# q and k of two token chunks by seven block products instead of eight, and the gate's logits out of v's products, on one core

## Chip, core and metric

The kernel runs on one core of a Trainium2 chip. The core has five engines with an instruction queue each: TensorE (PE in the profile; its weight loads are PEld), VectorE (DVE), ScalarE (ACT), GpSimd (POOL), and SyncE (SP), which here only issues DMAs. Each queue runs strictly in order, and semaphores tie the queues to each other. The metric is the device time of one execution in microseconds, median over several runs.

## What is computed

Input x has 2048 tokens of D = 448 features. Two branches are mixed token by token by a gate:

```python
g = sigmoid((x * gate_w).sum(-1, keepdims=True))
# branch A: attention over 8 keys, offsets 0, 2, .. 14 back; 16 heads of 28
q, k, v = split(x @ wqkv)                      # 448 x 1344
idx  = pos[:, None] - arange(8) * 2            # masked where < 0
o    = softmax(q . k[idx] * 28**-0.5) . v[idx]
a    = o @ wo
# branch B
b = relu(x @ w1 + b1)**2 @ w2 + b2             # 448 -> 1792 -> 448
return g * a + (1 - g) * b
```

All is fp32.

## The kernel before

Every fp32 product is made of three products in TensorE's faster 32-bit format: each operand is split into a high part (a rounded copy, on ScalarE) and a low part (raw minus high, on VectorE; `split_full`, L115 and L116), and hi x hi, hi x lo, lo x hi are summed in PSUM. The contraction over 448 features is three full blocks of 128 rows and an end of 64 rows (tiles `x7`, `x8`, weights `w7h`, `w7l`).

The matmuls run as pairs of 64-row halves of the array, side by side (`side_by_side`, L186): the two halves work on different accumulators at the same time. A block of 128 rows so takes one half product on the lower rows and one on the upper rows. An accumulator that has gathered the rows of one half must be handed to the other half; between the two a "turn" stands (`turn`), an operation on one element of the PSUM bank (memset on VectorE, L196, or a copy on ScalarE, L194) which waits for the first half's matmuls and for which the other half's matmuls wait.

Tokens come in four chunks of 512 (four tiles of 128). For each chunk TensorE makes q, k and v. Chunk 0 (`qkv_first`): 36 matmuls over full rows for q (L255), 48 pairs for the rest of q and for k, 42 pairs for v; v's turns stand after 24 pairs (v0, v1) and after 33 (v2, v3), counted as they are needed. Chunks 1 to 3: `qkv_two` twice, for two token tiles each, 63 pairs. Results go from PSUM into stage tiles on ScalarE (`qkv_evacuate`, L205, two token tiles to a stage tile, three stage tiles in all) and from there by DMA (L211) to q_d, k_d and v_d in DRAM. From there GpSimd's attention loads them (from 70.9 us on, products L335 and L342 on GpSimd, sums L336 and L350 on VectorE), while TensorE goes on with branch B ("h" and "b" matmuls) and at the end with the output product ("a").

The gate's logits are made on VectorE: for each chunk four multiplications of x's raw blocks by the gate's weights (L682, L680), a transposition (L686) and a sum (L687); they go through a small DRAM tile once.

The order of all instructions is fixed in the code: `when(t, ...)` puts a step in at an estimated time t (ns, of a clock that `advance` moves on with each group of matmuls), and steps that are due are written into the engines' queues between the matmuls. So what stands before what on an engine follows from these numbers. SP issues all DMAs in one queue; each issue also waits for the landing of the one eight places before it.

Of the kernel before, what the change touches and what calls it, by code (L numbers as in the profile page):

```python
# [14 lines left out]
P = 128  # L15
NS = 8
# [7 lines left out]
NQ = D + 2  # L24
NZ = 64
NP = 512
# [31 lines left out]
def gated_mix_kernel(ctx: ExitStack, tc: tile.TileContext, xT, wqkv, w1, w2, wo, b1, b2, out):  # L58
# [11 lines left out]
    z_d = tc.dram_tile([P, NZ], F32, name="z_d")  # L70
# [10 lines left out]
    w1h = const.tile([P, 3, F], F32R, name="w1h")  # L81
    w1l = const.tile([P, 3, F], F32R, name="w1l")
# [8 lines left out]

    xpool = ctx.enter_context(tc.tile_pool(name="xpool", bufs=1))
# [5 lines left out]
    zg = smallp.tile([P, 6, NS], F32, name="zg")  # L98
    zt, gt, g1t = zg[:, 0:2], zg[:, 2:4], zg[:, 4:6]
# [54 lines left out]
    wqh = ap.tile([P, 3, NP + 2 * D], F32R, name="wqh")  # L154
    wql = ap.tile([P, 3, NP + 2 * D], F32R, name="wql")

    w7h = ap.tile([P, NP + D], F32R, name="w7h")
    w7l = ap.tile([P, NP + D], F32R, name="w7l")
# [3 lines left out]
    nc.gpsimd.memset(halo0, 0.0)  # L162

    stage = {}

    def block(b):

        o = (0, NP, NP + D)[b]
        return slice(o, o + D)
# [29 lines left out]
    def qkv_evacuate(pt, c, tl, b):  # L199
        par, t = c // 2, (c % 2) * 4 + tl  # L200
        first = (b, t // 2) not in stage
        if first:
            stage[b, t // 2] = xap.tile([P, G, 2, C], F32, tag="stage", name=f"st{c}_{tl}_{b}", bufs=ST_BUFS)
        st = stage[b, t // 2]
        nc.scalar.activation(st[:, :, t % 2], pt[:, :D].rearrange("p (g c) -> p g c", g=G), AF.Copy)  # L205
        if not first:
            stage.pop((b, t // 2))
            t0 = t - t % 2
            dst, off = ((q_d, 0), (k_d, HALO), (v_d, HALO))[b]
            dd = dst[par, :, off:off + SP].rearrange("g (p s) c -> p g s c", s=NS)[:, :, t0:t0 + 2]  # L210
            nc.sync.dma_start(dd.rearrange("p g s c -> p g (s c)"), st.rearrange("p g s c -> p g (s c)"))  # L211
# [9 lines left out]
    def last(x, acc, tl, b):  # L221

        sl = slice(tl * P, tl * P + P)
        n = block(1) if b == 2 else slice(0, D)
        h, l = w7h[:, n], w7l[:, n]
        return [(acc, x.x7[:, sl], h), (acc, x.x7[:, sl], l), (acc, x.x8[:, sl], h)]

    def accs(c, b, tls, tags):
        return [Acc(t, f"qkv{c}_{tl}_{b}", D) for t, tl in zip(tags, tls)]
# [60 lines left out]


# [101 lines left out]
    def gates(par):  # L393

        e = smp.tile([P, 32], F32, tag="e", name=f"e{par}")[:, :NS]
        nc.scalar.activation(e, zt[:, par], AF.Exp, scale=-1.0)
# [127 lines left out]
    def w1_piece(i, dt, gap):  # L524
# [74 lines left out]
    def h_turn(accs, f):  # L599
        touch(w1h[:, 2].rearrange("p (f n) -> p f n", n=P)[:, f:f + 2, 0:1])  # L600
# [35 lines left out]

    raws = [raw_tile("wqraw0")]
    rx = raw_tile("xraw0")
    for k in range(4):
        if k < 3:  # L640
            nc.sync.dma_start(raws[0][:, k, :NQ], wqkv[0, :, k])
        else:
            for b, rows in ((0, slice(0, 64)), (1, slice(64, P))):
                nc.sync.dma_start(raws[0][rows, k, :NQ], wqkv[b, rows, k])
# [3 lines left out]
    for b, tag in ((1, "k"), (2, "v")):  # L648
        raw = attp.tile([P, 3, D], F32, tag=tag, name=f"wqraw{b}")
        for k in range(3):  # L650
            nc.sync.dma_start(raw[:, k], wqkv[b, :, k, :D])
        raws.append(raw)
    raw7 = attp.tile([P, D], F32, tag="q", name="wqraw7")
    nc.sync.dma_start(raw7, wqkv[2, :, 3, :D])
# [16 lines left out]
    zs = smp.tile([P, 3, NZ], F32, tag="lg", name="zs")  # L671
    zu = xcp.tile([P, CH], F32, tag="zu", name="zu")
    zpart, zall, gw = zs[:, 0], zs[:, 1], zs[:, 2, 0:4]
    nc.vector.tensor_copy(gw, raws[0][:, :, D])

    def z_product(raw, k):

        r = slice(0, P if k < 3 else 64)
        if k:
            nc.vector.scalar_tensor_tensor(zu[r], raw[r, k], gw[r, k:k + 1], zu[r], op0=ALU.mult, op1=ALU.add)  # L680
        else:
            nc.vector.tensor_scalar_mul(zu, raw[:, 0], gw[:, 0:1])  # L682

    def z_sums(c):

        nc.vector.transpose(zu, zu)  # L686
        nc.vector.tensor_reduce(  # L687
            zpart.rearrange("p (b c t) -> p c t b", b=4, c=4)[:, c],
            zu.rearrange("p (t b r) -> p t b r", t=4, b=4), axis=AX.X, op=ALU.add)

    def z_store():

        nc.sync.dma_start(z_d, zpart)

    def z_load():

        for b in range(4):
            nc.sync.dma_start(
                zall[b * 32:b * 32 + 32].rearrange("p (a n) -> p a n", a=4),
                z_d[:, b * 16:b * 16 + 16].rearrange("(a c) n -> c a n", a=4))  # L700

    def z_last():

        nc.vector.tensor_reduce(
# [516 lines left out]
```

## Time and profile before

| what | value |
|---|---|
| median of 3 runs | 413.39 us (413.04 to 413.75) |
| span of the profiled execution | 412.0 us; the page gives no other time of it, its runs' median is 1.4 us above |
| PE busy | 407.8 us, 99%, clock granted in full throughout |
| DVE, ACT, POOL busy | 270.6 (66%), 210.4 (51%), 268.4 (65%) us |
| DMA | 73.83 MB, mean 179 GB/s over the span |
| q, k, v of chunk 0 on PE | 4.34 to 31.28 us |
| all of q, k, v on PE | until 104.76 us, the last chunk mixed with other work from then on |

A row of the timeline reads: start, duration (of several instructions from the first's start to the last's end), engine, line, operation, output tile <- input tiles, shapes, count, and in brackets the idle time of the engine before it and what ended that. A row of the windows reads: stretch, its length, busy time and count of each engine, TensorE's clock, the DMA engines' busy share, GB/s.

### The profile page before, as it was taken

The numbers are of one execution on the slowest core, as the hardware profiler recorded it, in microseconds if no ns is written. First come the engines' busy times: TensorE is split into PE (matmuls) and PEld (weight loads), VectorE is DVE, ScalarE is ACT, GpSimd is POOL, SyncE is SP. The second block draws the span as 40 slices with busy tenths as digits, with TensorE's granted clock in tenths as the row PEclk, the third lists the DMA queues.
The fourth block names the chain that finished last, engine by engine and source line by source line (L and its number), as shares of the span: only waits on it lengthen the run. The fifth ranks groups of instructions, "written<-read, shape, count | busy, mean of one in ns | idle before, by whom it ended". The sixth has DMA issues, their size and how long they took to land.

```text
span 412.0 us, 9331 instructions
## 1 busy us (share of the span) xinstructions
PE 407.8 (99%) x3835; PEld 366.0 (89%) x3835; DVE 270.6 (66%) x430; ACT 210.4 (51%) x461; POOL 268.4 (65%) x167
## 2 busy tenths in 40 slices
PE   8999999999999999999999999999999999999997
PEld 7999999999888888888888888989898888888996
DVE  4590745276767766787656798879576677892354
ACT  4641646387775555444565535444653254346540
POOL 0000001955999999989989899999899977940000
PEclk9999999999999999999999999999999999999999
DMA  7999999979262315654112649765146530168304
GB/s 213 368 351 309 286 390 288 355 223 315 91 241 99 128 51 209 208 186 152 41 47 105 222 158 270 196 146 154 28 157 200 217 130 2 45 179 132 95 0 181
DMA packets 66763, 73.83 MB, mean 179 GB/s; under 512 B 33120, under 2 KB 59296, under 8 KB 66464
## 3 DMA queue, kind: packets, MB, share of 16 engines
q1 hardware_dynamic: 66720, 73.23, 55.4%
q8 instruction: 30, 0.49, 0.5%
q14 instruction: 13, 0.11, 0.1%
HBM read 45.74 MB, written 28.28 MB: 180 GB/s over the span
## 4 chain that ended last, share of the span: by engine, by line
PE 99%; DVE 0%; issue 0%
PE b L186 33%; PE h L186 32%; PE qkv L186 23%; PE a L186 7%; PE qkv L255 2%; PE warm L634 1%; PE a L993 1%; PE last L993 0%; DVE bt L872 0%; PE last L985 0%; PE a L985 0%; DVE zero L631 0%; DVE b1z L632 0%
## 5 line engine op out<-in xcount | busy, mean ns | idle before, releaser
L335 POOL TENSOR_TENSOR qk<-q,k 128x896 f32<-128x896 f32 x64 | 135.2, 2144 | 84.2 <-DMA k<-k_d 76.0
L342 POOL TENSOR_TENSOR av<-lg,v 128x896 f32<-128x896 f32 x64 | 119.2, 1957 | 6.2 <-DVE lg L336 5.6
L621 DVE TENSOR_TENSOR h<-h,h 128x512 fp32r<-128x512 f32 x56 | 38.4, 688 | 66.8 <-ACT h L624 66.5
L186 PE MATMUL qkv<-wqh,x 64*128 64x448 f32 x528 | 78.2, 359 | 0.0
L336 DVE TENSOR_REDUCE lg<-qk 128x32 f32<-128x896 f32 x64 | 67.0, 1074 | 0.0
L350 DVE TENSOR_REDUCE o<-av 128x112 f32<-128x896 f32 x64 | 66.4, 1070 | 0.1
L186 PE MATMUL b<-w2ah,h 64*128 64x448 f32 x448 | 66.3, 359 | 0.0
L186 PE MATMUL b<-w2bh,h 64*128 64x448 f32 x448 | 66.1, 359 | 0.0
L622 ACT ACTIVATE h<-h,b1z 128x512 f32<-128x512 f32 x56 | 36.7, 655 | 43.6 <-PE h L186 43.6
L186 PEld LDWEIGHTS qkv<-wqh,x 64*128 64x128 f32 x528 | 49.4, 184 | 3.6
L186 PE MATMUL qkv<-wql,x 64*128 64x448 f32 x264 | 47.7, 358 | 0.0
L186 PEld LDWEIGHTS b<-w2bh,h 64*128 64x128 f32 x448 | 42.1, 184 | 3.5
L186 PEld LDWEIGHTS b<-w2ah,h 64*128 64x128 f32 x448 | 42.0, 184 | 3.7
L205 ACT ACTIVATE st<-qkv 128x448 f32<-128x448 f32 x48 | 23.5, 542 | 34.3 <-PE qkv L186 31.7
L186 PE MATMUL b<-w2bl,h 64*128 64x448 f32 x224 | 40.7, 358 | 0.0
L186 PE MATMUL b<-w2al,h 64*128 64x448 f32 x224 | 40.5, 358 | 0.0
L623 ACT ACTIVATE h<-h 128x512 fp32r<-128x512 f32 x56 | 33.5, 598 | 1.7
L624 ACT ACTIVATE h<-h 128x512 f32<-128x512 f32 x56 | 33.3, 594 | 0.0
L573 ACT ACTIVATE h<-h 128x4 fp32r<-128x4 f32 (+1 forms) x35 | 7.2, 207 | 44.4 <-PE b L186 44.2
L186 PE MATMUL h<-x2b,w1h 64*128 64x512 f32 x168 | 28.1, 386 | 0.0
L186 PE MATMUL h<-x,w1h 64*128 64x512 f32 x168 | 28.1, 386 | 0.0
L186 PE MATMUL h<-x1b,w1h 64*128 64x512 f32 x168 | 28.1, 386 | 0.0
(150 smaller groups left out, 688.6 us busy)
## 6 DMA issues: line engine op xcount, KB each, us to landing
k<-k_d SPq DMA_DIRECT2D x8, 840.0 KB, 5.6
v<-v_d SPq DMA_DIRECT2D x8, 840.0 KB, 5.0
x_d<-x SPq DMA_DIRECT2D x11, 512.0 KB, 6.8
q_d<-st SPq DMA_DIRECT2D x8, 448.0 KB, 5.5
k_d<-st SPq DMA_DIRECT2D x8, 448.0 KB, 5.2
v_d<-st SPq DMA_DIRECT2D x8, 448.0 KB, 5.8
w1raw<-w SPq DMA_DIRECT2D x4, 896.0 KB, 9.2
q<-q_d SPq DMA_DIRECT2D x8, 448.0 KB, 3.6
```

The source lines that it names most:

```text
L186: nc.tensor.matmul(acc.pt[:, :acc.n], a[rows], w[rows], start=acc.todo == acc.all, stop=acc.todo == 1)
L205: nc.scalar.activation(st[:, :, t % 2], pt[:, :D].rearrange("p (g c) -> p g c", g=G), AF.Copy)
L255: nc.tensor.matmul(acc.pt[:, :D], a, w, start=k == j == 0, stop=False)
L335: nc.gpsimd.tensor_mul(pr, q[:, s:s + 1].to_broadcast([P, W, C]), k[:, s:s + W])
L336: pending.append(lambda: nc.vector.tensor_reduce(lg[:, s], pr.rearrange("p w (h d) -> p w h d", h=HG), axis=AX.X, op=ALU.add))
L342: nc.gpsimd.tensor_mul(pr.rearrange("p (h d) w -> p w h d", h=HG), lg[:, s][:, :, :, None].to_broadcast([P, W, HG, DH]), v[:, s:s + W].rea ...
L350: nc.vector.tensor_reduce(o[:, g * C:(g + 1) * C], pr, axis=AX.X, op=ALU.add)
L573: nc.scalar.activation(ap, f32(ap), AF.Copy)
L621: nc.vector.tensor_sub(hl, pt, f32(hh))
L622: ops += [lambda pt=pt, r=r: nc.scalar.activation(pt, pt, AF.Relu, bias=b1t[:, f + r:f + r + 1]), lambda pt=pt, hh=hh: nc.scalar.activatio ...
L623: lambda pt=pt, hh=hh: nc.scalar.activation(hh, pt, AF.Square),
L624: lambda pt=pt, r=r, low=low: (nc.scalar.activation(pt, pt, AF.Square), at(delays[r], low))]
```

## The change

For chunks 1 and 2, q and k of two token tiles are made together by Strassen's scheme. Take two token tiles (rows) and two weight blocks q and k (columns), and as the halves of the contraction the lower and the upper 64 rows of each 128-row block: a product of 2x2 blocks that takes eight block products, and by the scheme seven, of sums and differences of blocks. The sums of x's blocks (S: tiles `s`, from raw x and a second copy `xs` with its 64-row halves exchanged) and of the weights' blocks (T: from raw weights and an exchanged copy `tw`; and `t_ends` for the 64-row end) are made on chip and then split into high and low parts. T's parts lie in the tiles of w2's first part, which are free until later; S's in new half-width tiles that the second half of w1 takes later. The seven products and v's are run by `flow`, which goes through both chunks in one list with orders written by hand: each step has a half product on the lower and one on the upper rows, as the list and the accumulators' state allow. A unit of two tiles has 75 half products of q and k instead of 84; the PE queue has 468 half products in 237 steps for both chunks, six steps with one half empty (before: 504 in 252). Some results are added from PSUM to a stage tile on VectorE.

v's weights get two more columns with the gate's weights, so v's products are 450 wide in all chunks; ScalarE copies the logits' column out of PSUM, and the zu work and the way through DRAM go. Chunk 1's splits, the spills of x (x_d), w1's and w2's pieces get other times; the raw slot of x is taken ahead of that of q's weights.

The core of the diff:

```diff
-NQ = D + 2
...
+NV = D + 2
...
+    def qk_seven(c, u, x, inner):   # one unit: token tiles t[0], t[1] of chunk c; three banks X_, Y, Z
...
+        # bank, half of the rows, half products, which, waits for, gives, delay, what follows
+            one(X_, 0, 9, lambda: half_rows(0, *xt(0), *w_(0)), [], "s1", READ, lambda: copied(X_, "q", 0)),
+            one(Y, 1, 9, lambda: half_rows(1, *xt(0), *w_(0)), [], "y", TURN, lambda: turned(Y)),
+            one(Z, 0, 9, lambda: half_rows(0, *s_(1), *t_(0)), ["S"], "p5", READ, lambda: copied(Z, "k", 1)),
+            one(X_, 1, 9, lambda: half_rows(1, *s_(1), *t_(1)), ["s1", "p5"], "u2", READ, lambda: copied(X_, "k", 0)),
+            one(Y, 0, 3, lambda: ends(0, x, t[0], w7), ["y", "s1"], "c11", READ, lambda: added(Y, "q", 0), ...),
+            one(Z, 0, 3, lambda: ends(0, x, t[0], d7), ["p5"], "z", TURN, lambda: turned(Z)),
+            one(Z, 1, 9, lambda: half_rows(1, *s_(0), *w_(1)), ["z", "u2"], "c12", READ, lambda: added(Z, "k", 0), ...),
+            one(X_, 0, 12, lambda: half_rows(0, *s_(0), *t_(1)) + ends(0, x, t[1], d7), ["u2"], "c22", READ, lambda: added(X_, "k", 1), ...),
+            one(X_, 1, 12, lambda: half_rows(1, *xt(1), *t_(0)) + ends(1, x, t[1], d7), ["c22"], "c21", READ, lambda: copied(X_, "q", 1), ...),
...
+    def added(bank, b, r):
+        nc.vector.tensor_add(st[b][:, :, r], heads(bank.pt), st[b][:, :, r])
...
+    tw = [xpool.tile([P, 2, D], F32, tag=f"x{j}", name=f"tw{j}") for j in range(3)]
+    for j in range(3):
+        for to, of in ((slice(0, 64), slice(64, P)), (slice(64, P), slice(0, 64))):
+            nc.sync.dma_start(tw[j][to], wqkv[0:2, of, j, :D].rearrange("b p n -> p b n"))
+    def t_low(j):
+        q, k = raws[0][:, j, :D], raws[1][:, j, :D]
+        nc.gpsimd.tensor_sub(tw[j][LOW, 1], tw[j][LOW, 1], k[LOW])
+        nc.gpsimd.tensor_sub(tw[j][LOW, 0], k[LOW], q[LOW])
+    def t_high(j):
+        q, k = raws[0][:, j, :D], raws[1][:, j, :D]
+        nc.vector.tensor_sub(tw[j][HIGH, 1], k[HIGH], tw[j][HIGH, 1])
+        nc.vector.tensor_add(tw[j][HIGH, 1], tw[j][HIGH, 1], tw[j][HIGH, 0])
+        nc.vector.tensor_sub(tw[j][HIGH, 0], q[HIGH], tw[j][HIGH, 1])
+    def t_ends():
+        nc.vector.tensor_sub(raw7[HIGH, 1, :D], raw7[HIGH, 1, :D], raws[0][HIGH, 3, :D])
+        split_full(raw7[:, 1, :D], w2ah[:, 6], w2al[:, 6])
+    def t_split(j):
+        split_full(tw[j], w2ah[:, 2 * j:2 * j + 2], w2al[:, 2 * j:2 * j + 2])
+    def s_load(c):
+        for u in range(2):
+            xsum[c, u] = halfp.tile([P, 3, 2 * P], F32, tag=f"e{4 + u}", name=f"xs{c}_{u}")
+            for to, of in ((slice(0, 64), slice(64, P)), (slice(64, P), slice(0, 64))):
+                nc.sync.dma_start(xsum[c, u][to], xT[c, of, 0:3, u * 2 * P:(u + 1) * 2 * P])
+    def s_sums(c, u):   # four operations of 384 columns (128 or 64 rows) on GpSimd
...
+    s_load(1)
     for k in range(3):
         wq_split(1, k)
...
-    when(17900.0, z_sums, 0)
+    for j in range(3):
+        when(12000.0, t_low, j)
+    for u in range(2):
+        when(12500.0, s_sums, 1, u)
+    when(18600.0, t_ends)
+    for j in range(3):
+        when(18700.0 + j * 1300.0, t_high, j)
+        when(18700.0 + (j + 1) * 1300.0, t_split, j)
+    for u in range(2):
+        when(25500.0 + u * 4000.0, s_split, 1, u)
-    SPLIT_AT = {1: 19000.0, 2: 35000.0, 3: 53500.0}
+    SPLIT_AT = {1: 15000.0, 2: 34000.0, 3: 52000.0}
-    when(10500.0, x_spill, 0, x)
+    when(21000.0, x_spill, 0, x)
...
-    for c in range(4):
...
+    qkv_first(xs[0])
+    flow([(1, Later(1), True, FIRST), (2, Later(2), True, SECOND)], chunk_done)
```

Three places show how the queues change. First VectorE's, from the splits of chunk 1's x (`x1_...`) to the turns of chunk 0's v (`qkv0_<tile>_2`); before:

```order
L687 TENSOR_REDUCE zs_193<-zu_194 128x4x4 [waits DVE_49]
L116 TENSOR_TENSOR x1_0_421<-xraw1_196,x1_0_421 128x512 [waits DMAHW1_49,Activation_49]
L682 TENSOR_SCALAR zu_194<-xraw1_196,zs_193 128x512 [waits DVE_49]
L116 TENSOR_TENSOR x1_1_422<-xraw1_196,x1_1_422 128x512 [waits DMAHW2_49,Activation_49]
L196 MEMSET qkv0_0_2_384 1x1 [waits PE_49]
L196 MEMSET qkv0_1_2_385 1x1 [waits PE_49]
```

The same queue after, from the low part of x1's last block on (`w2al<-wqraw7` is the end of T, `tw0` to `tw2` its tiles):

```order
L130 TENSOR_TENSOR x1_3_386<-xraw1_199,x1_3_386 128x512 [waits DMAHW6_49,Activation_49]
L910 TENSOR_TENSOR wqraw7_169<-wqraw7_169,wqraw0_150 64x448 [waits DMAHW2_49]
L130 TENSOR_TENSOR w2al_75<-wqraw7_169,w2ah_74 128x448 [waits DMAHW1_49,Activation_49]
L905 TENSOR_TENSOR tw0_204<-wqraw1_161,tw0_204 64x448 [waits DMAHW0_49]
...
L907 TENSOR_TENSOR tw0_204<-wqraw0_150,tw0_204 64x448 [waits DVE_49]
L130 TENSOR_TENSOR w2al_75<-tw0_204,w2ah_74 128x896 [waits DMAHW7_49,Activation_49]
L905 TENSOR_TENSOR tw1_205<-wqraw1_161,tw1_205 64x448 [waits DMAHW2_49]
...
L907 TENSOR_TENSOR tw1_205<-wqraw0_150,tw1_205 64x448 [waits DVE_49]
L211 MEMSET qkv0_0_2_419 1x1 [waits PE_49]
L211 MEMSET qkv0_1_2_420 1x1 [waits PE_49]
L130 TENSOR_TENSOR w2al_75<-tw1_205,w2ah_74 128x896 [waits DMAHW1_49,Activation_49]
...
L211 MEMSET qkv0_2_2_421 1x1 [waits PE_49]
```

The turns now stand behind T's end, the low part of T's first tile and the operations on the second (each tile has a third operation, L906, left out here); the turn of v2 and v3 also behind the low part of the second and the operations on the third.

ScalarE's queue around the copies of chunk 0's k (`st0_<tile>_1`), before:

```order
L205 ACTIVATE st0_0_1_356<-qkv0_0_1_247 128x4x112 [waits DVE_49,PE_49]
L205 ACTIVATE st0_2_1_358<-qkv0_2_1_249 128x4x112 [waits DMAHW5_49,DVE_49,Activation_49]
L205 ACTIVATE st0_0_1_356<-qkv0_1_1_248 128x4x112 [waits DVE_49,PE_49]
L205 ACTIVATE st0_2_1_358<-qkv0_3_1_250 128x4x112 [waits DVE_49]
L115 ACTIVATE x1_0_421<-xraw1_196 128x512 [waits DMAHW1_49]
```

And after:

```order
L233 ACTIVATE st0_0_1_389<-qkv0_0_1_265 128x4x112 [waits DVE_49,PE_49]
L233 ACTIVATE st0_2_1_391<-qkv0_2_1_267 128x4x112 [waits DMAHW1_49,DVE_49,Activation_49]
L129 ACTIVATE x1_1_384<-xraw1_199 128x512 [waits DMAHW4_49]
L129 ACTIVATE x1_2_385<-xraw1_199 128x512 [waits DMAHW5_49]
L233 ACTIVATE st0_0_1_389<-qkv0_1_1_266 128x4x112 [waits DVE_49,PE_49]
L233 ACTIVATE st0_2_1_391<-qkv0_3_1_268 128x4x112 [waits DVE_49]
L129 ACTIVATE x1_3_386<-xraw1_199 128x512 [waits DMAHW6_49]
L129 ACTIVATE w2ah_74<-wqraw7_169 128x448 [waits DVE_49]
L129 ACTIVATE w2ah_74<-tw0_204 128x896 [waits DMAHW0_49,DMAHW7_49,DVE_49,Pool_49]
L129 ACTIVATE w2ah_74<-tw1_205 128x896 [waits DMAHW2_49,DVE_49,Pool_49]
```

In both the second copy waits for a DMA: it takes the stage tile that the first q store (st0_0_0) must have left. The splits of x1 now stand among the copies, and the high parts of T behind them.

SP's queue up to the first q store, before:

```order
L565 DMA xraw1_196<-xT 128x512 [waits DMAHW3_49]
L565 DMA xraw1_196<-xT 128x512 [waits DMAHW4_49]
L211 DMA q_d_57<-st0_0_0_258 128x4x224 [waits DMAHW5_49,Activation_49]
L211 DMA q_d_57<-st0_2_0_281 128x4x224 [waits DMAHW6_49,Activation_49]
L142 DMA x_d_60<-x0_0_167 128x1024 [waits DMAHW7_49]
L142 DMA x_d_60<-x0_1_168 128x1024 [waits DMAHW0_49]
```

And after:

```order
L763 DMA xraw1_199<-xT 128x512 [waits DMAHW6_49]
L896 DMA tw0_204<-wqkv 64x2x448 [waits DMAHW7_49]
L896 DMA tw0_204<-wqkv 64x2x448 [waits DMAHW0_49]
L896 DMA tw1_205<-wqkv 64x2x448 [waits DMAHW1_49]
L896 DMA tw1_205<-wqkv 64x2x448 [waits DMAHW2_49]
L896 DMA tw2_206<-wqkv 64x2x448 [waits DMAHW3_49]
L896 DMA tw2_206<-wqkv 64x2x448 [waits DMAHW4_49]
L923 DMA xs1_0_213<-xT 64x3x256 [waits DMAHW5_49]
L923 DMA xs1_0_213<-xT 64x3x256 [waits DMAHW6_49]
L923 DMA xs1_1_216<-xT 64x3x256 [waits DMAHW7_49]
L923 DMA xs1_1_216<-xT 64x3x256 [waits DMAHW0_49]
L225 DMA q_d_57<-st0_0_0_276 128x4x224 [waits DMAHW1_49,Activation_49]
```

Ten loads for T and S now stand between the last load of xraw1 and the first store of q; two 64-row loads of 448 columns into `wqraw7` (the ends for T) stand ahead of xraw1's.

More of the change, by code (lines that the diff above doesn't have):

```diff
@@ L23 @@
 CH = 512
-NQ = D + 2
-NZ = 64
-NP = 512
+NV = D + 2
+NB = 512
 SCALE = float(DH) ** -0.5
@@ L729, in x_begin @@
         if c == 1:
-            xs[c] = X(own, [prodp.tile([P, W * C], F32R, tag="pp", name=f"x{c}_3{n}", bufs=PP_BUFS)[:, 48:48 + CH]
-                            for n in range(2)])
+            xs[c] = X(own + [xpool.tile([P, 2, CH], F32R, tag="x3", name="x1_3")])
             return
```

334 lines of the change are left out of this document (245 added, 89 removed).

## Prediction, made before the changed kernel ran

> **What bounds the kernel now.** I read the busy line and the chain's shares on the page first, then the chain in order of time.
>
> ```profile
> span 412.0 us, 9331 instructions
> PE 407.8 (99%) x3835; PEld 366.0 (89%) x3835; DVE 270.6 (66%) x430; ACT 210.4 (51%) x461; POOL 268.4 (65%) x167
> PE 99%; DVE 0%; issue 0%
> 13.21 91.55 PE qkv L186 x912
> ```
>
> TensorE is the whole chain: it has work from 1.2 us to the end and waits for nothing. So every step less on it is worth its time, but only while no other engine or transfer becomes late for it; and every wait that the change puts in front of it counts in full. The last row prices a step: 912 matmuls are 456 pairs (two 64-row halves side by side) in 91.55 us, 0.2008 us a pair. The span is 412.0 us, the median of the runs 413.39, so 1.4 us lie outside the span; I add differences to the median.
>
> Chunk 0 is unchanged on TensorE, so its times are known: 48 pairs for q and k from 13.21, hence v starts at 13.21 + 48 x 0.2008 = 22.85. After 24 pairs of v, at 27.67, TensorE needs the turn of v0 and v1, after 33 pairs, at 29.47, that of v2 and v3. A turn is a one-element memset on VectorE, which runs its instructions in order. So I look at what VectorE does there:
>
> ```profile
> 20.11 0.48 DVE L682 TENSOR_SCALAR zu<-xraw,zs 128x512 f32<-128x512 f32 x1
> 20.63 2.32 DVE L680 SCALAR_TENSOR_TENSOR zu<-xraw,zs,zu 128x512 f32<-128x512 f32 x3
> 22.98 0.71 DVE L686 STREAM_TRANSPOSE zu<-zu 128x512 f32<-128x512 f32 x1
> 23.73 0.69 DVE L687 TENSOR_REDUCE zs<-zu 128x16 f32<-128x512 f32 x1
> 26.28 0.06 DVE L196 MEMSET qkv<- 1x1 f32 x2
> 28.78 0.73 DVE L680 SCALAR_TENSOR_TENSOR zu<-xraw,zs,zu 64x512 f32<-64x512 f32 x1
> 28.84 0.06 DVE L196 MEMSET qkv<- 1x1 f32 x2
> ```
>
> The turns were done at 26.34 and 28.90, only 1.3 and 0.6 us before they were wanted. There is almost no slack at this place, and the order shows that the change puts a chain of three engines ahead of these very memsets.
>
> **The TensorE work.** Of chunks 1 and 2, 504 half matmuls in 252 steps become 468 in 237 steps (six halves stay empty): 15 x 0.2008 = -3.01 us. The v products grow from 448 to 450 columns in 168 pairs: 168 x 0.2008 x 2/448 = +0.15. Sum **-2.86 us**.
>
> **The gate.** The change takes from VectorE the zu rows above, for each chunk 0.48 + 4 products of about 0.74 + 0.71 + 0.69, and z's way through memory; ScalarE gets 16 one-column copies. Neither engine is on the chain; cost nothing, covered by the 34% and 49% in which they are idle. It matters only as 4.8 us less in VectorE's queue between 20 and 25.
>
> **When the first q store lands.** New loads stand in SP's queue between the loads of xraw1 and the first stores of q: raw7's second part 2 x 115 KB (ahead of xraw1), the six of tw 229 KB each, four of xs1 197 KB each, together 2.39 MB.
>
> ```profile
> 12.25 1.75 SPq L565 DMA_DIRECT2D xraw<-xT  x4
> 15.34 1.45 SPq L211 DMA_DIRECT2D q_d<-st  x2
> q_d<-st SPq DMA_DIRECT2D x8, 448.0 KB, 5.5
> 8.50:10.40 1.90, 1.90 (x11) 1.78 (x10) 1.69 (x5) 1.26 (x4) 0.00 (x0) 1.00 1.04 318
> 10.40:12.20 1.80, 1.80 (x11) 1.69 (x10) 1.45 (x5) 1.78 (x4) 0.00 (x0) 1.00 1.07 382
> wqraw<-wqkv SPq DMA_DIRECT2D x3, 225.0 KB, 4.1
> wqraw<-wqkv SPq DMA_DIRECT2D x2, 112.5 KB, 5.6
> ```
>
> The store was issued at 15.34 and took about 5.5: landed near 20.8. In the two windows the last two columns are the busy share of the DMA engines, full, and the GB/s. The first holds the two loads into 64 rows that the kernel has today, the kind of which the change adds twelve, so I take its 318: 2.39 MB / 318 = 7.5 us, landing **28.3**. Ends: at 382 GB/s 27.1; if loads into 64 rows cost twice their bytes (the last two rows show half the bytes taking no less time, 5.6 against 4.1 us), about 35.
>
> Who waits for it: there are three stage tiles, so the fourth, for tile 2's k, needs the first q store landed. ScalarE waits there with everything behind it.
>
> ```profile
> 21.26 0.98 ACT L205 ACTIVATE st<-qkv 128x448 f32<-128x448 f32 x2 [3.00 <-PE qkv L186]
> 23.06 0.98 ACT L205 ACTIVATE st<-qkv 128x448 f32<-128x448 f32 x2 [0.82 <-PE qkv L186]
> 23.93 2.19 ACT L115 ACTIVATE x<-xraw 128x512 fp32r<-128x512 f32 x4
> ```
>
> Before, the store was home at about 20.8, just ahead of the copy at 21.26, whose wait was for TensorE. After, this copy starts at 28.3.
>
> **The chain to the memset of v0 and v1.** In the changed order ScalarE still has two splits of x1, two copies, the last split of x1, the ends of T, and the first T tile; VectorE's memset stands behind the low part of x1_3, t_ends with its low part, t_high(0), the low part of T tile 0, and t_high(1). Prices:
>
> ```profile
> L116 DVE TENSOR_TENSOR x<-xraw,x x13: 677/686/704, 11.4 to 61.9; 128x512 fp32r<-128x512 f32 x13
> L116 DVE TENSOR_TENSOR wql<-wqraw,wqh x6: 617/618/625, 12.1 to 18.3; 128x448 fp32r<-128x448 f32 x6
> L115 ACT ACTIVATE x<-xraw x13: 614/632/654, 10.7 to 59.3; 128x512 fp32r<-128x512 f32 x13
> L115 ACT ACTIVATE w7h<-wqraw x2: 565/571/577, 10.2 to 17.7; 128x448 fp32r<-128x448 f32 x2
> L736 ACT ACTIVATE x<-x x3: 1050/1050/1052, 70.5 to 72.4; 128x1024 fp32r<-128x1024 f32 x3
> L1035 POOL TENSOR_TENSOR w2bl<-w2raw,w2bh x2: 1151/1154/1157, 121.8 to 125.3; 128x448 fp32r<-128x448 f32 x2
> 5.86 1.59 PE L255 MATMUL qkv<-wqh,x 128*128 128x448 f32 x4
> 9.05 0.96 PE L255 MATMUL qkv<-wqh,x 128*128 128x448 f32 x4
> ```
>
> From 28.3: copy 0.49 (half of 0.98), two splits of 0.55 (a fourth of 2.19), two copies 0.98, last split 0.63: 31.5. VectorE 0.69 and t_ends 0.62: 32.8. ScalarE 0.57, VectorE 0.62: 34.0. t_high(0) is three 64x448 operations; on VectorE 64 partitions took as long as 128 (0.73 at 28.78 above, against 2.32 for the three at 20.63, most of them 128 high), so 3 x 0.62: 35.9. ScalarE 128x896, between 0.63 for 512 columns and 1.05 for 1024: 0.95, 36.8. VectorE 128x896, twice 0.62: 38.1. t_high(1) 1.86: 39.9; memset 40.0. Against 27.67 TensorE waits **12.3 us**. With the ends of the landing the wait is 11.1 or 19.
>
> GpSimd works from about 20 on: six t_low at 1.15 and eight sums of 384 columns at 1.15 x 384/448 = 0.99, 14.8 us, to about 35. In this profile GpSimd's first arithmetic is at 70.89 (the row below), so nothing shows a VectorE subtraction of two SBUF tiles beside GpSimd's there. Bounds: 0, if they don't disturb each other; +5, if each waits for the other until GpSimd is through (about 4 us of its work left when the chain starts at 31.5, 1 us before). I take **+2**: 14.3 us.
>
> ```profile
> 70.89 12.59 POOL L335 TENSOR_TENSOR qk<-q,k 128x896 f32<-128x896 f32 x6 [69.51 <-DMA k<-k_d]
> ```
>
> **The second turn.** TensorE has nine pairs, 1.8 us, between the turns; VectorE's next memset stands behind the low part of T tile 1 (1.24) and t_high(2) (1.86), and the low part behind ScalarE's 0.95: 4.05 us. TensorE waits 4.05 - 1.8 = **+2.25**. After such a pause TensorE may run slowly: the two rows of the start show four matmuls in 1.59 us at 5.86 and in 0.96 at 9.05. Bounds 0 and 1.6 (the nine pairs at twice 0.2, of which a part falls into the second wait); I take **+0.8**. The Trainium skill (TensorE: Matmul & The Clock Gate, Part 1: The HAM clock gate) says that the array falls to half clock after an idle window of about 3.4 us and needs about 3.4 us of work to get back, which agrees with the slow rows at the start; by it, an estimate, the penalty is up to 1.7 us, the upper end.
>
> **Afterwards.** The loops of chunks 1 and 2 wait for nothing more by my reckoning: GpSimd's and VectorE's sums for chunk 1 follow during the stall; the xraw2 load goes out behind a v store and lands about 5.4 us after the loop's start, wanted at 8.5; chunk 2's sums are on GpSimd from 8 to 16 us after it. Attention starts about 36.5 us after the loop's start, against 39.7 from chunk 1's start now (70.89 - 31.28, the end of v's 42 pairs), with 3.0 us less TensorE work behind it: no loss. Each of these is cheap because the stall itself gives them the time.
>
> Sum: -2.86 + 14.3 + 2.25 + 0.8 = **+14.5 us**: 412.0 to 426.5 in the span, 413.39 to **427.9** in the runs.
>
> **Rivals.**
> 1. ScalarE isn't held: the store lands in time, since the loads are spread over many DMA engines or are quick. Then the chain starts with the copies at 24.0; x1_3's split 24.7, its low part 25.4, and on as above, memset at 33.1: wait 5.4, +2.25, -2.86 = +4.8, **418.2**. For it: the row of 382 GB/s; against it: the DMA engines are full in both windows. 12%.
> 2. VectorE and GpSimd take full turns: +5 instead of +2, **430.9**. The Trainium skill (SBUF — State Buffer, § Who interferes with whom) has it that a VectorE instruction with two SBUF inputs and a GpSimd one that reads SBUF exclude each other for a whole instruction; no run here shows it yet. For it as a mechanism of this kernel: nearly all of the chain's VectorE work has two such inputs. 20%.
> 3. Loads into 64 rows at half the rate: landing 35 instead of 28.3, wait +6.7, of which GpSimd's disturbance falls away (-2): **432.6**. For it the 112.5 KB row; against it the 318 GB/s. 12%.
> 4. The other side: no wait on TensorE, **410.5**. This needs the first memset by 27.67 + 2.86 - 2.25 = 28.3, nearly 12 us earlier than I reckon and 4.8 earlier than even rival 1. It decides if VectorE's queue isn't behind T's chain, for instance because half-height operations take half the time and ScalarE runs far ahead. 4%.
> 5. Attention, shifted by the stall, ends too late for the output product. Of its last loads those issued from 364.44 are used by ScalarE at 378.36; issue 1.75 and 3.1 to landing give 369.3, 9 us of slack, and TensorE behind it is shifted alike, save the 3.0 us saved. Nothing to add; it would give 429. 3%.
>
> ```profile
> 364.44 1.75 SPq L923 DMA_DIRECT2D ot<-o_d  x3
> ot<-o_d SPq DMA_DIRECT2D x24, 128.0 KB, 3.1
> 378.36 0.84 ACT L942 ACTIVATE oh<-ot 128x768 fp32r<-128x768 f32 x1
> ```
>
> **Numbers.** My forecast has 49%, so 427.9 us. From 417 (rival 1, with a smaller second wait) to 435 (rivals 2 and 3 together with a cold TensorE) holds all but rival 4 and a few mixtures. A measurement of this kernel can tell about 0.2%, 0.8 us, from no change. Faster: rival 4, 4%. Same, from a stall of about 2 to 3.6 us, below every case but 4: 2%. Slower: 94%.
>
> **What would show it.** In the waits, TensorE's v matmuls of chunk 0 waiting for VectorE's memset for 12 to 17 us from 27.7, and a second time for 2 to 3 us; ScalarE's copy into the stage waiting for the q store to about 28; TensorE's rows right after the wait longer than 0.36 us; the loop of chunks 1 and 2 taking 237 x 0.2008 = 47.6 us without a wait; VectorE's t_high rows at 0.62 us (or longer beside GpSimd). The prediction is wrong if the memset comes by 28, or if the loads of tw land so late that GpSimd's t_low holds ScalarE instead, or if the loop itself waits for its additions on VectorE.

## The result, and the profile after

The changed kernel takes 444.04 us (median of 4, 443.82 to 444.55) against 413.32 beside it: ratio 1.0743, 95% interval 1.0728 to 1.0758, +30.7 us. The sign and the place of the largest loss are as forecast; the size is twice the forecast 14.5, and outside the range given (417 to 435).

From the page of after, its span, its engines and the chain that ended last:

```profile
span 442.2 us, 9347 instructions
PE 412.1 (93%) x3799; PEld 368.2 (83%) x3799; DVE 282.6 (64%) x426; ACT 218.3 (49%) x489; POOL 292.6 (66%) x189
PE 68%; DMA 14%; POOL 9%; SPq 2%; issue 2%; ACT 2%; DVE 2%; ACTq 0%; POOLq 0%
```

TensorE has its 36 matmuls fewer (3799 for 3835) and is 93% busy where it was 99%: it now waits. From the waits (us in total, times, longest), the three largest of TensorE, and from its timeline, in order, each pause above 0.3 us up to h and the first matmuls of three stages; the bracket holds the pause and what ended it:

```profile
PE qkv L201 <- DVE qkv L211: 21.4, 4, 16.0
PE qk_z L470 <- ACT st_k L363: 1.3, 1, 1.3
PE v L470 <- ACT st_q L363: 1.2, 1, 1.2
```

```profile
43.71 0.74 PE L201 MATMUL qkv<-wqh,x 64*128 64x450 f32 x2 [16.04 <-DVE qkv L211]
47.84 0.74 PE L201 MATMUL qkv<-wqh,x 64*128 64x450 f32 x2 [0.39 <-DVE qkv L211]
50.42 0.40 PE L470 MATMUL v<-wqh,x 64*128 64x450 f32 x2
82.94 0.47 PE L470 MATMUL v<-wqh,x 64*128 64x450 f32 x1 [1.24 <-ACT st_q L363]
86.37 0.47 PE L470 MATMUL qk_z<-w2ah,x 64*128 64x448 f32 x1 [1.35 <-ACT st_k L363]
102.19 0.56 PE L201 MATMUL qkv<-wqh,x 64*128 64x448 f32 x3
111.87 0.47 PE L201 MATMUL qkv<-wqh,x 64*128 64x448 f32 x2 [2.23 <-DVE qkv L211]
116.68 0.47 PE L201 MATMUL qkv<-wqh,x 64*128 64x448 f32 x2 [2.72 <-DVE qkv L211]
132.28 0.40 PE L201 MATMUL h<-x,w17h 64*128 64x512 f32 x2
437.98 1.01 PE last L1235 x9
```

The first two are the forecast turns of v0, v1 and v2, v3. The loop of chunks 1 and 2 starts at 50.42, chunk 3 at 102.19, the first h matmul at 132.28; the last row, of the chain, ends TensorE's work at 438.99. Before, in the same two places:

```profile
104.60 0.40 PE L186 MATMUL h<-x,w17h 64*128 64x512 f32 x2
407.98 1.02 PE last L993 x9
```

So TensorE ends 30.0 us later, and this divides. Steps saved, 15 x 0.2008: -3.0. From 27.67, where the forecast put the wait's start, to the loop: 22.75 us for 18 pairs worth 3.6: +19.1. The loop: 51.77 for 237 x 0.2008 = 47.6: +4.2, of which 2.8 are pauses. Chunk 3 up to h: 30.09 for 113 pairs worth 22.7: +7.4, of which the two pauses are 4.95. The rest: 306.7 against 304.4: +2.3. The sum is +30.0.

The same matmuls remain from chunk 3's start on in every kernel of this study, so their times can be set side by side (us at which the matmul starts that has so many left, itself counted, from the traces' rows; the first mark lies within a pair or two of chunk 3's start; the names are those of the experiments below):

| left | before | after | e5 | e4 | e3 | e9 | e10 | e11 | e8 |
|---|---|---|---|---|---|---|---|---|---|
| 3100, chunk 3 starts | 81.86 | 102.19 | 81.81 | 98.67 | 94.76 | 102.65 | 81.24 | 80.97 | 95.52 |
| 2874, at the first h | 104.60 | 132.28 | 104.70 | 128.61 | 123.17 | 126.69 | 105.26 | 110.90 | 123.11 |
| 2700 | 123.49 | 151.24 | 123.67 | 147.57 | 143.44 | 148.33 | 125.81 | 129.87 | 149.01 |
| 2500 | 144.61 | 174.41 | 144.79 | 170.84 | 166.84 | 171.01 | 149.34 | 152.77 | 170.13 |
| end | 408.98 | 438.98 | 409.36 | 435.41 | 431.41 | 435.87 | 414.55 | 417.34 | 435.35 |

**The long pause.** Three rows of SyncE, ScalarE and VectorE show how it comes about, the timeline of after in order of time:

```profile
14.48 4.06 SPq L896 DMA_DIRECT2D tw<-wqkv  x6
18.58 4.15 SPq L923 DMA_DIRECT2D xs<-xT  x4
23.11 1.24 SPq L225 DMA_DIRECT2D q_d<-st  x2
29.44 0.54 ACT L233 ACTIVATE st<-qkv 128x448 f32<-128x448 f32 x1 [7.92 <-DMA q_d<-st]
34.16 1.30 DVE L910 TENSOR_TENSOR wqraw<-wqraw,wqraw 64x448 f32<-64x448 f32 x1
36.83 1.30 DVE L905 TENSOR_TENSOR tw<-wqraw,tw 64x448 f32<-64x448 f32 x1
43.57 0.06 DVE L211 MEMSET qkv<- 1x1 f32 x2
47.70 0.06 DVE L211 MEMSET qkv<- 1x1 f32 x2
```

The ten loads of T and S are issued ahead of the q stores (14.48 to 22.7); ScalarE's copy of tile 2's k is let go by a q store at 29.44 after 7.92 us of idleness; T's end (L910) and T's first tile (L905) follow on VectorE, and the memset that TensorE waits for is at 43.57.

### The profile page after: what moved, and what is told of

Same layout as the page of the kernel before. It is cut to its first block, busy times and chain, and to the rows that moved or that the text cites. A ratio compares the mean times of both kernels' runs of the same rounds, so it can differ in the third digit from the quotient of the medians.

```text
span 442.2 us, 9347 instructions
## 1 busy us (share of the span) xinstructions
PE 412.1 (93%) x3799; PEld 368.2 (83%) x3799; DVE 282.6 (64%) x426; ACT 218.3 (49%) x489; POOL 292.6 (66%) x189
## 4 chain that ended last, share of the span: by engine, by line
PE 68%; DMA 14%; POOL 9%; SPq 2%; issue 2%; ACT 2%; DVE 2%; ACTq 0%; POOLq 0%
PE b L201 28%; PE h L201 26%; PE a L201 7%; POOL qk L529 6%; POOL av L536 3%; DMA w1raw<-w 2%; PE qk_x L470 2%; PE v L470 2%; DMA v_d<-st 2%; DMA q_d<-st_q 2%; DMA k<-k_d 2%; DMA tw<-wqkv 2%; PE qk_z L470 2%; DMA q_d<-st 1%; DMA xraw<-xT 1%
## 5 line engine op out<-in xcount | busy, mean ns | idle before, releaser
L823 DVE TENSOR_TENSOR h<-h,h 128x512 fp32r<-128x512 f32 x56 | 38.6, 689 | 58.4 <-ACT h L826 58.3
L201 PE MATMUL qkv<-wqh,x 64*128 64x448 f32 (+1 forms) x240 | 41.3, 391 | 21.4 <-DVE qkv L211 21.4
L201 PEld LDWEIGHTS qkv<-wqh,x 64*128 64x128 f32 x240 | 26.8, 202 | 24.7 <-DVE qkv L211 23.1
L201 PE MATMUL b<-w2al,h 64*128 64x448 f32 x224 | 40.5, 358 | 0.0
L201 PE MATMUL qkv<-wql,x 64*128 64x448 f32 (+1 forms) x120 | 25.8, 386 | 0.0
L470 PE MATMUL v<-wqh,x 64*128 64x450 f32 x96 | 23.1, 364 | 1.2 <-ACT st_q L363 1.2
L130 DVE TENSOR_TENSOR x<-xraw,x 128x512 fp32r<-128x512 f32 x13 | 12.6, 1009 | 17.9 <-ACT x L129 17.6
L201 PEld LDWEIGHTS b<-w2bl,h 64*128 64x128 f32 x224 | 21.1, 184 | 1.9
L201 PEld LDWEIGHTS b<-w2al,h 64*128 64x128 f32 x224 | 20.9, 184 | 2.0
```

Source lines behind the costliest of these rows:

```text
L130: soon(lambda: nc.vector.tensor_sub(lo, raw, f32(hi)))
L201: nc.tensor.matmul(acc.pt[:, :acc.n], a[rows], w[rows], start=acc.todo == acc.all, stop=acc.todo == 1)
L470: nc.tensor.matmul(q["bank"].pt[:, :q["bank"].n], a, w, start=new, stop=i == len(q["prods"]) - 1, skip_group_check=True)
L823: nc.vector.tensor_sub(hl, pt, f32(hh))
```

## Experiments on the early pause

e1 to e4, and e7 and e9 below, are one run each. The kernels that ran four or five times spread by 0.7 to 2.1 us, so differences of 3 us and more are read here, and pauses from the traces.

**e1_own_stage**: chunk 0's k gets tiles of its own, so ScalarE isn't held by the store.

```diff
-                qkv_evacuate(acc.pt, c, tl, b)
+                qkv_evacuate(acc.pt, c, tl, b, c == 0 and b == 1)
```

> Chunk 0's k gets stage tiles of its own (free product tiles), so ScalarE no longer waits for the first q store; nothing else moves. Theory A (the early pause is VectorE's chain of T in front of the turns, started late by ScalarE's hold): the splits of x1 come about 7 us earlier, the first pause falls from 16.0 to about 9.5 us, about 437.5 us in all. Rival (the T loads and GpSimd set the chain, the hold hides behind them): pause stays above 14, about 443. Theory B on the later pauses (they only follow from the early one): they shrink with it, below 430.

440.47 us (before 412.98 beside it). The pause shrank to 12.66, not to 9.5. Freed earlier, the chain simply ran through all of GpSimd's sums (GpSimd busy 21.2 to 40.5): from the copy of tile 2's k (20.84) to the memset it took 18.8 us, where after has 14.1 (29.44 to 43.57).

```profile
28.64 1.44 DVE L905 TENSOR_TENSOR tw<-wqraw,tw 64x448 f32<-64x448 f32 x1
39.63 0.06 DVE L211 MEMSET qkv<- 1x1 f32 x2
```

The store's hold was thus worth some 3.5 us by itself, and the chain behind it is the larger part. Chunk 3's two pauses stay (2.79 and 1.03).

**e2_late_t**: T's steps are put behind the turns.

```diff
-    when(18600.0, t_ends)
+    when(22100.0, t_ends)
     for j in range(3):
-        when(18700.0 + j * 1300.0, t_high, j)
-        when(18700.0 + (j + 1) * 1300.0, t_split, j)
+        when(22200.0 + j * 1300.0, t_high, j)
+        when(22200.0 + (j + 1) * 1300.0, t_split, j)
```

> T's steps on VectorE and ScalarE are put behind the turns of chunk 0's v; the hold of ScalarE stays. Theory A: first pause only up to x1's last low part, about 6.5 us, no second pause, but the turns of chunk 1's v and the products of T then wait for the same chain at the start of the seven-product loop, about 8 us there: about 440 us. Rival (T isn't needed so early, only its place in the queue cost time): no new pause in the loop, about 432 us.

440.23 us. The first pause fell to 5.83, the second went; a new one of 4.95 stood in the loop, in front of a step that waits for the turn of `qk_y`, a memset behind the splits of T and S in VectorE's queue.

**e3_both**: both edits together.

> Both edits: own stage tiles for chunk 0's k, and T behind the turns. Theory A: no pause at 27.7 us, but TensorE reaches chunk 1 at 31 us and the chain of T and S ends at about 44, so about 8 us of pause in the loop instead; 433 us. If the late pauses (chunk 3, 5 us and slow rows) follow from the early one, 425; if they have a cause of their own they stay and the time is about 433.

436.38 us. No pause is left in chunk 0, but one of 10.45 us in the loop, from 38.6 us:

```profile
PE v L470 <- DVE qk_y L374: 10.5, 1, 10.5
```

L374 is again the turn of `qk_y`. In these three runs the pause moves from one turn to another and shrinks by some 6 us at most. The step that this turn lets go reads no T; the first product that does (`qk_z` with `w2ah`) starts eleven pairs later, which from 38.6 is about 40.8, while T's last split on VectorE ended at 47.96. So some of the 10.45 us is the turn's place in the queue and the rest, some 7 us, would by this be a wait for T itself; no run separates the two.

**e4_no_pool**: after, without GpSimd's sums (`t_low`, and `s_sums` for chunk 1).

```diff
-    for j in range(3):
-        when(12000.0, t_low, j)
-    for u in range(2):
-        when(12500.0, s_sums, 1, u)
```

> GpSimd's part of T and the sums S of chunk 1 are left out (those sums are not made); all else as in the changed kernel. Theory A with full turn-taking between VectorE and GpSimd: the lows of x1 and T's subtractions of two tiles fall from 1.2-1.3 to 0.6-0.7 us, first pause 13 us instead of 16, about 441 us. Rival (these VectorE rows are long for another reason, such as full DMA queues): rows stay at 1.2, pause stays at 16.

440.38 us, the first pause 11.06 (it begins 1.9 us later than in after, since this execution's chunk 0 was late from its start, so the chain is compared and not the pause). The same chain without GpSimd beside it:

```profile
32.53 0.62 DVE L910 TENSOR_TENSOR wqraw<-wqraw,wqraw 64x448 f32<-64x448 f32 x1
40.45 0.06 DVE L211 MEMSET qkv<- 1x1 f32 x2
```

The subtraction takes 0.62 us instead of 1.30, the memset comes 3.1 us sooner. Of these, 0.6 is the store: ScalarE's copy was let go at 28.81 here. From that copy to the memset the chain takes 11.64 us, against 14.13 in after, so GpSimd costs it 2.5 us, between the +2 taken and the +5 of rival 2. Where all of the chain lies beside GpSimd's sums (e1, 18.8 us) it costs 7.2, more than rival 2's price. The Trainium skill (SBUF — State Buffer, § Who interferes with whom) lets a VectorE instruction with two SBUF inputs and a GpSimd one that reads SBUF exclude each other for a whole instruction; by that, an instruction is lengthened by up to one of the other engine's, and the rows agree. An addition with one of its two inputs in PSUM ran beside such GpSimd sums at half of 1.18 us, as with GpSimd idle (two in 1.19 at 84.65); in the timeline of after:

```profile
60.69 4.39 DVE L130 TENSOR_TENSOR x<-xraw,x 128x512 fp32r<-128x512 f32 x3 [0.32 <-DMA xs<-xT]
65.78 1.18 DVE L366 TENSOR_TENSOR st_q<-qk_y,st_q 128x448 f32<-128x448 f32 x2 [0.57 <-DMA x_d<-x]
```

The three splits ahead of it, both inputs in SBUF, took 4.39 us, 1.46 each, where the rows of before have 0.69.

## The gate alone

**e5_gate_only**: no seven products; only the gate's part of the change (v 450 wide), with the load and split times of before.

```diff
-    flow([(1, Later(1), True, FIRST), (2, Later(2), True, SECOND)], chunk_done)
+    for c in (1, 2):
+        qkv_two(xs[c], c, 0)
+        qkv_two(xs[c], c, 2)
+        chunk_done(c)
...
-    s_load(1)
-    for j in range(3):
-        when(12000.0, t_low, j)
...
```

> The gate's part of the change alone: logits from two more columns of v's products, zu rows and z's way through memory gone; all chunks by eight products, steps at the times of the kernel before. By the sum 168 pairs x 0.2008 x 2/448 = +0.15 us, nothing else: 413.1 to 413.2 beside 413.0, no pause on TensorE. Rival: the sixteen one-column copies on ScalarE stand ahead of the copies that free accumulators, a pause per chunk, above 414.

414.74 us (414.42 to 415.29) against 413.42, ratio 1.0035 (1.0021 to 1.0048): +1.3 us. TensorE has no new pause. The chain's row for all q, k, v products, against 13.21 and 91.55 us for the same 912 before:

```profile
12.63 92.23 PE qkv L201 x912
```

+0.68, against the 0.15 that 450 for 448 columns would give. The profiled execution (414.42, the quickest of them) ends TensorE's work 0.38 us later than before's, and its span is 0.6 longer; the page of before doesn't say which run it shows, so where the rest of the 1.3 goes stays open. The rival's time (above 414) came about, its pauses did not. The work taken from VectorE brought no time back, as forecast.

## Seven products for one chunk only

**e6_one_chunk**: chunk 1 by eight (`qkv_two`), chunk 2 by seven, in an order of 117 steps; T's loads after the q stores, T made over the time of chunk 1.

```diff
-    for j in range(3):
-        for to, of in ((slice(0, 64), slice(64, P)), (slice(64, P), slice(0, 64))):
-            nc.sync.dma_start(tw[j][to], ...)
+    when(11500.0, t_load)
-    when(18600.0, t_ends)
+    when(23500.0, t_ends)
     for j in range(3):
-        when(18700.0 + j * 1300.0, t_high, j)
+        when(24000.0 + j * 2500.0, t_high, j)
...
-    when(25000.0, x_more, 2)
+    when(31500.0, x_more, 2)
...
```

> Only chunk 2 by seven products (chunk 1 by eight), T's loads after the first q stores and T's steps spread over chunk 1, a new hand-written order for one chunk in 117 steps instead of 126: -1.8 us, gate +0.15. Theory A: with 25 us more for T and S there is no early pause, 411.4 us if nothing waits late. If the late pauses come from stage tiles in the product buffers (still used for chunk 2 here), up to 5 us of them stay around the start of chunk 3 and 414 to 417 results. Rival (the seven-product loop waits by itself for its additions on VectorE): pauses within the loop, above 416 too, but before chunk 3.

442.58 us, ratio 1.0712 (1.0694 to 1.0730), far from both times expected. Other queues now carried the wait: 5.37 us where chunk 1's turn stood behind a `t_high`; 6.61 us at 79.6 because the copy that TensorE waited for stood in ScalarE's queue behind a split of w1, which waited for w1's load. That load was issued at 72.31, behind 2 MB of x_d:

```profile
85.12 0.58 ACT L129 ACTIVATE w1ah<-w1raw 128x448 fp32r<-128x448 f32 x1 [9.22 <-DMA w1raw<-w]
```

Two more pauses, 3.45 and 1.01 us, are chunk 3's turns.

**e8_one_chunk_spread**: the same with T spread further, stage tiles of their own, and other tiles for chunk 2's raw x, so that none of these waits should occur.

```diff
-            return prodp.tile([P, G, 2, C], F32, tag="pp", name=name, bufs=PP_BUFS)
+            spare[0] += 1
+            return xpool.tile([P, G, 2, C], F32, tag=f"x{spare[0] % 3}", name=name)
...
+    when(10400.0, t_load)
...
-            at(12000.0 + j * 2000.0, lambda j=j: nc.scalar.activation(xm[c].t[j], f32(own[j]), AF.Copy))
+            at(26500.0 + j * 1500.0, lambda j=j: nc.scalar.activation(xm[c].t[j], f32(own[j]), AF.Copy))
...
```

> Again only chunk 2 by seven products, in 117 steps instead of 126, but T's and S's steps are placed between the turns of chunk 1, no load that waits for a buffer stands ahead of a store in SP's queue, and chunk 2's stage tiles lie in tiles of their own instead of the attention's product buffers. Theory: every pause of the other kernels came from a turn or a stage copy queued behind such a wait, not from the seven products; then no pause over 0.5 us is left, and the time is that of the gate's part alone (414.7) less nine steps, 1.8 us: 412.9. Rival (the loop waits by itself for VectorE's additions or its stage tiles): pauses inside the loop of chunk 2, 3 us or more, 416 and above.

440.90 us (439.57 to 441.69), ratio 1.0664 (1.0639 to 1.0689): far from the 412.9 I had expected. It lost 13.7 us by chunk 3's start, 4.8 within chunk 3, 7.0 soon after. One of its pauses, 3.17 us in the loop, stands behind VectorE rows that lie beside GpSimd's attention, in the timeline of e8:

```profile
75.65 8.82 POOL L531 TENSOR_TENSOR qk<-q,k 128x896 f32<-128x896 f32 x4 [25.26 <-DMA k<-k_d]
78.76 6.11 DVE L130 TENSOR_TENSOR w17l<-w1raw,w17h 64x128 fp32r<-64x128 f32 x4
```

The same four in after, with GpSimd idle:

```profile
74.72 1.16 DVE L130 TENSOR_TENSOR w17l<-w1raw,w17h 64x128 fp32r<-64x128 f32 x4
```

Four small subtractions take 1.16 us alone and 6.11 beside four products in a row, and the addition behind them on VectorE is late. The first three of them took 1.64, 2.11 and 2.05 us and each ended 0.15 us behind one of GpSimd's products (2.12 to 2.5 us each); the fourth, beside none, took 0.22. Another pause (4.55 us) was a turn of chunk 1 behind T's steps and the splits of the next x.

## Experiments on chunk 3 and the loop

In after, chunk 3's first two turns come late (the pauses of 2.23 and 2.72). The timelines of GpSimd, SyncE and VectorE there:

```profile
91.59 2.13 POOL L529 TENSOR_TENSOR qk<-q,k 128x896 f32<-128x896 f32 x1 [21.28 <-ACT w17h L129]
108.52 2.10 POOL L529 TENSOR_TENSOR qk<-q,k 128x896 f32<-128x896 f32 x1 [14.80 <-DMA k_d<-st_k]
110.65 1.08 DVE L530 TENSOR_REDUCE lg<-qk 128x32 f32<-128x896 f32 x1 [2.83 <-POOL qk L529]
111.67 0.64 DVE L714 TENSOR_TENSOR w1bl<-copy,w1bh 128x448 fp32r<-128x448 f32 x1
111.73 0.06 DVE L211 MEMSET qkv<- 1x1 f32 x2
87.06 1.98 SPq L156 DMA_DIRECT2D x_d<-x  x4
93.42 0.37 SPq L225 DMA_DIRECT2D k_d<-st_k  x1
93.88 3.38 SPq L722 DMA_DIRECT2D w1raw<-w  x2
97.36 1.55 SPq L225 DMA_DIRECT2D k_d<-st_k  x1
```

Some of the loop's stage tiles (v's, and k's of every second unit of two token tiles) are GpSimd's product tiles. Attention's second product waits 14.80 us until a k store has left such a tile; the store (issued at 97.36, landed at 108.39) is behind 2 MB of x_d and 1.8 MB of w1. VectorE's sum of that product stands in its queue, and the one-element memset that TensorE waits for stands behind the sum.

The two pauses don't make up all of chunk 3's 7.4 us: from 117.6 to 121.0, right behind the second, nine pairs of matmuls took 0.37 us each instead of 0.20, another 1.6 us. The granted clock of that stretch (the figure behind the five engines' busy times) is below full, in the windows of after:

```profile
110.00:120.00 10.00, 5.41 (x40) 4.63 (x42) 6.28 (x17) 4.79 (x11) 7.27 (x5) 0.88 0.55 169
```

**e7_late_loads**: x_d's spill and w1's third and fourth pieces later, their loads and their splits.

```diff
-    when(57000.0, lambda: x_spill(2, xs[2]))
+    when(76000.0, lambda: x_spill(2, xs[2]))
-    when(64000.0, w1_piece, 2, 74400.0, 1450.0)
-    when(65000.0, w1_piece, 3, 80300.0, 1450.0)
+    when(75000.0, w1_piece, 2, 79500.0, 1450.0)
+    when(76500.0, w1_piece, 3, 86500.0, 1450.0)
...
```

> The changed kernel with chunk 2's spill of x and the loads of w1's second half put behind chunk 2's stores in SP's queue. Theory: chunk 3's pauses (2.2 and 2.7 us and the slow rows after) come from product buffers that are free only when chunk 2's stores have landed, and those land about 8 us late behind these transfers; then the pauses fall below 1.5 us together and the time to about 440. Rival (GpSimd and VectorE are simply late after the early pause, by their own work): pauses stay near 5 us, 444.

445.29 us. The k stores landed at 95.9 and 98.2, the second product ran at 98.32, and chunk 3's first turn was in time; but w1's split, ahead of another turn on VectorE, now waited for its own late load: 3.58 us.

**e9_late_loads_b**: as e7, with w1's third piece loaded early and split late.

```diff
-    when(57000.0, lambda: x_spill(2, xs[2]))
+    when(76000.0, lambda: x_spill(2, xs[2]))
-    when(64000.0, w1_piece, 2, 74400.0, 1450.0)
-    when(65000.0, w1_piece, 3, 80300.0, 1450.0)
+    when(60000.0, w1_piece, 2, 80400.0, 1450.0)
+    when(76500.0, w1_piece, 3, 86500.0, 1450.0)
...
```

> As the run with chunk 2's spill and w1's loads put behind the stores, but the third piece of w1 is loaded early, so that its copies on VectorE don't wait for it ahead of a turn. Theory (chunk 3's pauses are turns behind VectorE rows that wait for GpSimd, GpSimd for product buffers, these for late stores): both pauses of chunk 3 under 1 us together, about 439 us with the early pause still there. Rival: 5 us of pauses stay, 444.

440.84 us, -3.2. The k stores landed at 98.7 and 100.1, and the second product ran at 100.22. Chunk 3 up to h takes 24.0 us for 30.1, the early pause is there as in after; the waits of e9:

```profile
PE qkv L201 <- DVE qkv L211: 17.7, 3, 16.6
```

The chain of waits is confirmed for these pauses: with the stores early, the second product ran 8 us sooner and both pauses went (one of 0.74 us stands later, at 125.4). The edit also moves w1's splits; in the rows of after the memset comes at the end of the sum (111.73), not of the split beside it. Of the 6.0 us gained 2.7 are lost again in the next 174 matmuls (2874 to 2700 left: 21.6 us, before 18.9).

**e10_no_sums**: e9 without T's and S's sums, their loads and splits (the seven products run on plain blocks of x and weights).

```diff
-            return tuple(lambda j, n=n: S[c, u][n][:, j, r * P:r * P + P] for n in range(2))
+            return xt(r)
-            return (lambda j: w2ah[:, 2 * j + b]), (lambda j: w2al[:, 2 * j + b])
+            return w_(b)
...
-        when(12000.0, t_low, j)
-        when(12500.0, s_sums, 1, u)
-    when(18600.0, t_ends)
-        when(18700.0 + j * 1300.0, t_high, j)
-        when(18700.0 + (j + 1) * 1300.0, t_split, j)
...
```

> All sums are left out: no loads, subtractions and splits for T and S; the seven products take blocks of x and of the weights as they are (q and k of chunks 1 and 2 are not those of the reference), in the same order and number on TensorE, with the same additions to the stage tiles on VectorE; the late loads stand as in the run that removed chunk 3's pauses. Theory: the early pause was the sums alone, so 413.3 + 1.3 (gate's part) - 3.0 = 411.6, plus up to 3 us for the loop's waits for stage tiles: 411.6 to 414.6. Rival: the loop waits because of its nine products' order and its additions, not because of the sums: 420 and above.

418.81 us (417.98 to 419.98), ratio 1.0134 (1.0110 to 1.0158): above the 414.6 expected at most and below the rival's 420. **e11_no_sums_plain** is the same with after's times for the loads and w1's splits.

> The same without sums, but with the loads and the spill where the changed kernel has them. Theory (chunk 3's pauses are independent of the early one): they stay, about 5 us and slow rows after them, 418 to 422. Rival (they only follow from the early pause): gone with it, as fast as the run beside it.

422.85 us (421.87 to 423.23), ratio 1.0222 (1.0205 to 1.0239).

In both, the early pause is gone. Chunk 3 starts at 81.24 and 80.97, 0.6 to 0.9 ahead of before, but 0.4 to 0.6 of that lies ahead of the loop: from its first matmul (30.82, 30.62; before 31.26) it takes 50.4 us in each, against 50.6 before. So of the 3.0 us saved 0.2 is left even when the sums are free. In e10 the pauses are 0.50 and 1.34; the other 48.6 us make about 0.204 a step, where 0.2008 was reckoned (e5 has 0.2023 for a pair, 92.23 us for 456). In e11 chunk 3's two pauses are as in after (4.8 us), with no early pause ahead of them, so they don't come from it. The loop's pauses come from the stage tiles: ScalarE's copies wait for stores, as in after; the rows of e10:

```profile
60.96 0.98 ACT L363 ACTIVATE st_q<-qk_x 128x448 f32<-128x448 f32 x2 [2.59 <-DMA q_d<-st_q]
64.83 0.98 ACT L363 ACTIVATE st_k<-qk_z 128x448 f32<-128x448 f32 x2 [1.85 <-DMA q_d<-st_q]
```

Then e10 loses 1.3 us against before up to h, 1.7 up to 2700 left, 2.4 up to 2500 and 0.8 behind it. GpSimd's attention was somewhat behind over that time; the windows of before, then of e10 (busy time and count of PE, PEld, DVE, ACT, POOL, then PE's clock, DMA share and GB/s):

```profile
105.00:150.00 45.00, 45.00 (x424) 39.50 (x424) 30.45 (x42) 28.24 (x65) 44.23 (x28) 1.00 0.36 128
```

```profile
105.00:150.00 45.00, 42.75 (x388) 36.67 (x386) 31.01 (x43) 27.23 (x66) 40.68 (x26) 1.00 0.43 152
```

Every kernel with seven products in both chunks takes 22.7 to 23.5 us from 2700 to 2500 left; before, e5, e6 and e8 take 21.1. In after and e10 three short pauses at b stand there, behind VectorE's and ScalarE's work on h. Why that work is late by so much there wasn't tested.

By these runs the making of the sums (their loads, subtractions and splits) costs 444.0 - 422.9 = 21 us, the place of the loads 422.9 - 418.8 = 4, and the two columns of the gate 1.3 (e5). What then remains of e10's 5.4 above before, 4.1, is what the other waits cost beyond the 3.0 saved.

## Why the prediction was right in sign and wrong in size

- Saved steps: -2.86 with the gate's cost. The 15 steps went, but the gate alone costs 1.3, not 0.15, and the loop's steps were dearer than 0.2008 (e10). A term mis-sized by 1.1 or more.
- The landing of the first q store: 28.3; it landed at 29.3 and ScalarE went on at 29.44. Rival 1 (not held), rival 3 (half rate, 35) and rival 4 (no wait) are out. Of rival 5 there is no sign: TensorE's waits show none at the output product.
- The chain from the landing to the first memset: 11.7 us forecast, 11.6 in e4 without GpSimd. GpSimd's part: +2 taken, 2.5 measured. With the landing, 14.3 against 16.04. The mechanism of rival 2 holds, here at half of its price.
- The second turn and the cold array: 2.25 + 0.8 = 3.05; measured 19.1 - 16.0 = 3.1. The second memset came 4.13 us after the first (forecast 4.05), and the nine pairs between the turns ran slowly within that time, from 43.71 to 47.45, 3.74 us instead of 1.8, so only 0.39 was left to wait. Behind it nine pairs took 2.58 us instead of 1.8, the 0.8 allowed for. The granted clock was 0.61 and 0.53:

```profile
30.00:40.00 10.00, 0.00 (x0) 0.00 (x0) 8.14 (x8) 3.45 (x7) 7.26 (x6) 0.61 0.78 291
40.00:50.00 10.00, 5.91 (x32) 4.81 (x34) 7.13 (x13) 3.65 (x8) 0.00 (x0) 0.53 0.04 13
```

  The Trainium skill (TensorE: Matmul & The Clock Gate, Part 1: The HAM clock gate) puts the array at half clock after an idle window of about 3.4 us until some 3.4 us of work are done. The pace agrees (0.375 us a pair instead of 0.20), but the slow pairs last longer, from 43.71 to 49.1, and in chunk 3 the slow pairs follow pauses of 2.23 and 2.72 us.
- The step that failed is "Afterwards": "The loops of chunks 1 and 2 wait for nothing more by my reckoning", and for attention behind them "no loss". It cost 4.2 + 7.4 + 2.3 = 13.9 us, nearly all of the miss of 16. Attention's first product ran 41.2 us after the loop's start (91.59 - 50.42), not 36.5, and its second only at 108.52. I had followed the inputs of each step (loads, splits, sums) and the start of attention, but not the places that results are put in: some of the loop's stage tiles are attention's product tiles, their stores are behind other DMAs, and TensorE's turns are behind attention's sums on VectorE. e9, e10 and e11 show these links for chunk 3; the loop's pauses have the same cause by the rows (ScalarE's copies wait for stores), which no run tested by itself; why the matmuls behind h are late stays open. "Each of these is cheap because the stall itself gives them the time" was wrong: with the stall gone (e11), the pauses of chunk 3 are the same.

No version tried here beats the kernel before.

## What to carry to other kernels

A tiny operation that hands a buffer on, in an in-order queue, inherits every wait that stands ahead of it there; before moving work, list what is queued ahead of each such operation on each engine, and follow also where each result is put and when that place comes free. On an engine that is 99% busy a saving of 3 us must be paid for by work that has cover elsewhere: here making the sums, placed as they are, cost 21 us where they saved 3.

## What was not expected of the hardware

VectorE's subtraction of two SBUF tiles goes from 0.62 to 1.30 us beside GpSimd, and four small ones from 1.16 to 6.11 beside GpSimd's products in a row, while an addition with one input in PSUM stays at 0.59. After 16 us of idleness TensorE took 3.74 us for 1.8 us of work, and it also ran at that pace for nine pairs after two pauses of 2.2 and 2.7 us with 2 us of work between them.
